# Windowed attention ahead of a gated feed-forward: values of attention in quarters of the array, in two phases round the scores, and two blocks turned at once

## The chip, the cores and the metric

The kernel runs on one core of a Trainium2 chip. The metric is the device time of one execution in microseconds (us), as a median over runs. TensorE (PE in the profile) multiplies matrices, VectorE (DVE) and ScalarE (ACT) work elementwise on 128 partitions, SyncE (SP) issues transfers; each engine goes through its own instructions in order and waits for the others by semaphores. Matmul results land in PSUM, of which a partition has eight banks of 2 KB.

## The reference

Four batches of 768 tokens, 8 heads of 64; each token attends to itself and the 95 before it, and to the first 8 tokens of its sequence. The heads' outputs, 512 wide, go through a gated product and two matrices:

```python
scores = scale * np.matmul(q, k.transpose(0, 1, 3, 2))      # q, k, v: (4, 8, 768, 64), float32
is_global = pos[None, :] < int(n_global)                     # 8
is_local = (rel >= 0) & (rel < int(n_local))                 # 96
bias = -slopes[:, None, None] * dist[None, :, :]
scores = np.where(is_global | is_local, scores + bias[None], -1e9)
scores = scores - np.max(scores, axis=-1, keepdims=True)
a = np.exp(scores)
a = a / (np.sum(a, axis=-1, keepdims=True) + 1e-09)
x = np.matmul(a, v)              # then (3072, 512)
out = ((x @ w1) * (x @ w2) @ w3) @ w_out       # 512 -> 1024 -> 1024 -> 512
```

## The kernel before

**Tiling.** A chunk is 256 tokens (12 in all, 3 to a batch), a block 128 of them (j = 0, 1). Heads go in pairs; u is the head of a pair, and its 64 dimensions are one half of the partitions. A step `s` does two pairs of one chunk, so there are 24 steps. The queries of a block see at most 232 keys: a window of 96 and 8 global ones ahead (104 rows, the "window" piece of the keys), and the block itself (128, the "own" piece). The first block of a batch has no window, so it has only the own piece.

**A step.** PE writes the scores of two pairs (line 406) in 64x64 pieces, which use the four quarters of the array in turn: a half of the rows (u) by a half of the columns (the half g of the block's queries). A piece spans 168 columns, since each half of the queries sees no more; in a batch's first block 64 or 128. DVE adds the bias and takes the rows' extremum (line 421, eight instructions with a read of the accumulator each), ACT makes exponentials and sums (line 422), DVE and ACT scale the rows (lines 427 to 436). PE transposes them (lines 445 and 447) through a PSUM tile of a bank, one block of a pair at a time ("turn", four a step), and ACT copies the result `ph` to SBUF (line 449). PE then multiplies by the values `vr` (457 for the own piece, 459 for the window piece, summed in PSUM). The weights are 64 columns wide, one head's, so a matmul uses all rows (128 or 104) and half the columns. The result `uu`, 128 partitions by two pairs by 256 tokens in one bank, is split into a high part `xh` (ACT, line 63) and the rest `xl` (DVE, line 64). A float32 matmul shows as two records in the trace.

**Visits.** The values of step s - 1 and the scores of step s stand next to one another on PE; that stretch is called visit s here (0 to 24). Between visits PE runs slices of the feed-forward of earlier tokens: a generator (lines 150 to 186) yields after each piece of 6 matmuls, products with w1 and w2 (161 to 163; each in three, high by high, high by low, low by high), then with the folded w3 w_out (178 to 180). ACT evicts the first product (`a`, 168), DVE multiplies (`g`, 171), and ACT and DVE split the product into `gh` and `gl` (63, 64). A new run of the generator begins behind every fourth visit (8, 12, 16, 20; smaller runs before), when 512 tokens are complete.

**What sets the order.** PE's order is written out by hand throughout: the table `SLICES` says how many slices stand between a step's softmax and its turns. In steps 0 to 3 (`first_steps`) DVE's and SP's orders are written by hand too, since the weights are converted from 64-bit floats there (lines 54 to 58, 130, 147) and w3 w_out is folded on PE (142); ACT's order there is the scheduler's. From step 4 on ACT's order is the one in which the code stands, and the scheduler orders DVE and SP.

**PSUM** is full: four banks of scores, one for turns, one for values, two for the feed-forward.

Of the kernel before, what the change touches and what calls it, by code (L numbers as in the profile page):

```python
# [10 lines left out]
F32 = mybir.dt.float32  # L11
F32R = mybir.dt.float32r
BF16 = mybir.dt.bfloat16
I32 = mybir.dt.int32
AF = mybir.ActivationFunctionType
ALU = mybir.AluOpType
PSUM = bass.MemoryType.PSUM

B, H, S, D = 4, 8, 768, 64
DM, DF, DO = 512, 1024, 512  # L20
P = 128
NP = H // 2
NQ = 2
T = NQ * P
NCB = S // T
# [7 lines left out]
BW = WIN + GLB  # L33
UW = BW + P
QW = KW + T
STEP = 2
PC = 512
HF = NFC // 2
HQ = P // 2
# [27 lines left out]
class FeedForward:  # L67
# [25 lines left out]
    def next(self, ring, slots):  # L93
        self.turn[ring] += 1
        return slots[(self.turn[ring] - 1) % len(slots)]
# [229 lines left out]
def banded(ctx, tc, ff, ns, nt, nf, oki, ident, qk, vx):  # L325


    nc = tc.nc
# [3 lines left out]
    ld = ctx.enter_context(tc.tile_pool(name="ld", bufs=STEP))  # L332
    at = ctx.enter_context(tc.tile_pool(name="at", bufs=2))
    ps_s = ctx.enter_context(tc.tile_pool(name="ps_s", bufs=1, space=PSUM))
    ps_t = ctx.enter_context(tc.tile_pool(name="ps_t", bufs=1, space=PSUM))
    ps_v = ctx.enter_context(tc.tile_pool(name="ps_v", bufs=1, space=PSUM))
    sc = [[ps_s.tile([P, NQ, 256], F32, name=f"s{i}{u}") for u in range(2)] for i in range(STEP)]

# [4 lines left out]
    biasw = bp.tile([P, H, UW], BF16, name="biasw")  # L343

    def biases():
        it = at.tile([P, UW], I32, tag="ph", bufs=4, name="it")
        itg = at.tile([P, P], I32, tag="ph", bufs=4, name="itg")
        rel, loc = (at.tile([P, UW], F32, tag="pr", name=n) for n in ("rel", "loc"))

        dist, both0 = ff.t3s[:, 2].bitcast(F32)[:, :UW], ff.t3s[:, 3].bitcast(F32)  # L350
        keep0, dist0 = both0[:, :P], both0[:, P:2 * P]
        own = slice(BW, UW)
        nc.gpsimd.iota(it[:, 0:WIN], pattern=[[-1, WIN]], base=WIN, channel_multiplier=1)
        nc.gpsimd.iota(it[:, WIN:BW], pattern=[[1, GLB]], base=0, channel_multiplier=0)
        nc.gpsimd.iota(it[:, BW:UW], pattern=[[-1, P]], base=0, channel_multiplier=1)
        nc.gpsimd.iota(itg, pattern=[[1, P]], base=0, channel_multiplier=0)
        nc.vector.tensor_copy(out=rel, in_=it)
        nc.vector.tensor_copy(out=keep0, in_=itg)
        nc.vector.tensor_scalar(out=loc, in0=rel, scalar1=0.0, scalar2=None, op0=ALU.is_ge)
        nc.vector.tensor_copy(out=nf, in_=nt)  # L360
        nc.vector.scalar_tensor_tensor(out=loc, in0=rel, scalar=nl, in1=loc, op0=ALU.is_lt, op1=ALU.mult)
        nc.vector.tensor_scalar(out=loc[:, WIN:BW], in0=rel[:, WIN:BW], scalar1=ng, scalar2=None, op0=ALU.is_lt)
        nc.vector.tensor_tensor(out=dist, in0=rel, in1=loc, op=ALU.mult)
        nc.vector.tensor_scalar(out=dist[:, WIN:BW], in0=loc[:, WIN:BW], scalar1=nl, scalar2=None, op0=ALU.mult)

        nc.vector.scalar_tensor_tensor(out=keep0, in0=keep0, scalar=ng, in1=loc[:, own], op0=ALU.is_lt, op1=ALU.max)
        nc.vector.tensor_tensor(out=dist0, in0=keep0, in1=loc[:, own], op=ALU.subtract)
        nc.vector.scalar_tensor_tensor(out=dist0, in0=dist0, scalar=nl, in1=dist[:, own], op0=ALU.mult, op1=ALU.add)
        for d, m in ((dist0, keep0), (dist, loc)):
            nc.vector.tensor_scalar(out=m, in0=m, scalar1=-FAR, scalar2=FAR, op0=ALU.mult, op1=ALU.add)  # L370
            nc.vector.tensor_tensor(out=d, in0=d, in1=m, op=ALU.add)
        for h in range(H):
            sl = -SLOPES[h] / SCALE
            nc.scalar.activation(bias0[:, h, :], dist0, AF.Copy, scale=sl)
            nc.scalar.activation(biasw[:, h, :], dist, AF.Copy, scale=sl)
# [18 lines left out]
    def scores(c, hp, qr):  # L394

        ps = sc[hp % STEP]
        for j in range(NQ):
            w0 = BW if c % NCB == 0 and j == 0 else 0  # L400
            for g in range(P // HQ):
                cols = slice(max(w0, g * HQ), BW + (g + 1) * HQ)
                q0 = KW + j * P + g * HQ
                for u in range(2):
                    m = qr[u * D:(u + 1) * D]
                    nc.tensor.matmul(ps[u][g * HQ:(g + 1) * HQ, j, cols], lhsT=m[:, q0:q0 + HQ], rhs=m[:, j * SLOT:][:, cols], start=True, stop=True)  # L406
        return ps
# [28 lines left out]
                    nc.vector.tensor_scalar(out=x, in0=x, scalar1=r, scalar2=None, op0=ALU.mult)  # L436
        return pr

    def flip(c, hp, j, pr):

        first = c % NCB == 0 and j == 0
        nk = 1 if first else 2
        pt = ps_t.tile([P, 2, 2, P], F32, tag="t", name=f"t_{c}_{hp}_{j}")
        for u in range(2):
            nc.tensor.transpose(pt[:, u, 0], pr[:, j, u, BW:UW], ident)  # L445
            if not first:
                nc.tensor.transpose(pt[:, u, 1], pr[:, j, u, 0:P], ident)  # L447
        ph = at.tile([P, 2, 2, P], F32, tag="ph", bufs=4, name=f"ph_{c}_{hp}_{j}")
        nc.scalar.activation(ph[:, :, :nk], pt[:, :, :nk], AF.Copy)  # L449
        return ph  # L450

    def values(uu, c, hp, vr, phs):
        for j, ph in enumerate(phs):
            first = c % NCB == 0 and j == 0
            for u in range(2):
                rows, o = slice(u * D, (u + 1) * D), uu[u * D:(u + 1) * D, j * P:(j + 1) * P]
                nc.tensor.matmul(o, lhsT=vr[:, j, rows], rhs=ph[:, u, 0], start=True, stop=first)  # L457
                if not first:
                    nc.tensor.matmul(o, lhsT=vr[:BW, 2 * NQ - 1 - j, rows], rhs=ph[:BW, u, 1], start=False, stop=True)  # L459

    n = NC * NP // STEP
    pairs = lambda s: [divmod(STEP * s + i, NP) for i in range(STEP)]
    work = []
    qrs, vrs, phs, xs = {}, {}, {}, {}

    def slices(k):
        while k > 0 and work:
            if next(work[0], "end") == "end":  # L470
                work.pop(0)
            else:
                k -= 1
# [7 lines left out]
    def visit(s):  # L481
        if s:
            c, h0 = pairs(s - 1)[0]
            if h0 == 0 and c % 2 == 0:
                xs[c // 2] = [xp.tile([P, NCC, W], F32R, tag=tag, name=f"{tag}_{c}") for tag in ("xh", "xl")]
            uu = ps_v.tile([P, STEP, T], F32, tag="v", name=f"v_{c}_{h0}")
            for i, p in enumerate(pairs(s - 1)):
                values(uu[:, i], *p, vrs[s - 1][i], phs[s - 1][NQ * i:NQ * (i + 1)])
        ps = [scores(*p, t) for p, t in zip(pairs(s), qrs[s])] if s < n else []
        if s:  # L490
            x2 = xs[c // 2]
            xc = [x[:, :, c % 2 * T:][:, :, :T] for x in x2]
            split(nc, *(x[:, h0:h0 + STEP] for x in xc), uu)
            if h0 + STEP == NP and c < 2:
                work.append(ff.run(c, *xc, c * T, T))
            elif h0 + STEP == NP and c % 2:
                work.append(ff.run(c, *x2, (c - 1) * T, W))
        return ps
# [1 line left out]
    def all_rows(s, ps):  # L500
        return [rows(*p, x) for p, x in zip(pairs(s), ps)]

    def turn(s, m, prs):
        phs.setdefault(s, []).append(flip(*pairs(s)[m // NQ], m % NQ, prs[m // NQ][0]))

    def first_steps():

# [22 lines left out]
        ps = visit(0)  # L530
# [5 lines left out]
        prs = all_rows(0, ps)  # L536
# [12 lines left out]
            loads(s + 1)  # L549

        def fold_and_turn(f, s):
            for m in range(STEP * NQ):
                ff.fold(f, 2 * m, 2 * m + 1)
                turn(s, m, prs)

        w3(3)
        scale(0)
# [9 lines left out]
        prs = all_rows(1, visit(1))  # L567
# [11 lines left out]
        prs = all_rows(2, visit(2))  # L579
# [11 lines left out]
        prs = all_rows(3, visit(3))  # L591
# [4 lines left out]
        w12(7)  # L596
        slices(SLICES[3][0] - 2)
        ff.lows()
        for m in range(STEP * NQ):
            turn(3, m, prs)  # L600
            slices(SLICES[3][m + 1])
        fits(nc, ff.mp, nf, oki)


    SLICES = [()] * 3 + [(4, 2, 2, 1, 1)] * 3 + [(4, 2, 1, 1, 1)] * 2 + [(5, 2, 2, 2, 1)] * (n - 8)
    with tc.manual_schedule(engines={mybir.EngineType.PE}):
        with tc.manual_schedule(engines={mybir.EngineType.DVE, mybir.EngineType.SP}):
            first_steps()
        with tc.manual_schedule(engines={mybir.EngineType.Activation}):
            for s in range(4, n + 1):  # L610
                rs = all_rows(s, visit(s))
                if s == n:
                    break

                slices(2)
                for p, r in zip(pairs(s), rs):
                    softmax(*p, *r, nc.vector)
                loads(s + 1)
                slices(SLICES[s][0] - 2)
                for m in range(STEP * NQ):  # L620
                    turn(s, m, rs)
                    slices(SLICES[s][m + 1])
            slices(10 ** 6)


# [43 lines left out]
```

## Time and profile before

| | before |
|---|---|
| median of 3 runs | 600.2 us |
| lowest and highest run | 599.47, 601.7 us |
| span of the profiled execution, first to last instruction | 597.9 us (the page gives no time of its own beside it) |
| mean granted TensorE clock | 0.997 |
| busy: PE, DVE, ACT | 574.8, 261.2, 287.3 us |
| ACT copies of turned blocks, 128x512 or 128x256 | 96, 53.7 us |

A row of the timeline gives the start and the length of an instruction in us, its engine, line, operation and operands (out <- in), "x4" for four records of a kind in a row, and in brackets how long the engine was idle before it and what released it. The lengths of neighbouring matmuls overlap, since matmuls are pipelined, so a pace is read from starts. A row of the windows gives start and end, the length, and for each engine its busy time and its number of instructions, then the granted clock (1.00 is full), the share of DMA and GB/s. A row of the groups gives a line, an engine, an operation, names and shapes, a count, and after the bar the busy time in us and the mean in ns.

### The profile page before, as it was taken

Reading aid. Unit: us, or ns where it says so; the run is one execution under the profiler, and the core shown is the slowest. Engines: PE = TensorE matmul, PEld = TensorE weight load, DVE = VectorE, ACT = ScalarE, POOL = GpSimd, SP = SyncE. Lnnn points to the kernel's source line nnn. Section 1 sums busy time; section 2 is a strip of 40 time slices with the busy share of each in tenths; the row PEclk is TensorE's granted clock in tenths of the full one; section 3 lists DMA queues with packets and bytes.
Section 4 is the critical chain, followed back from the end, with each engine's and each line's share of the span. In section 5 each row is a group of like instructions: output and inputs, shape, how many; then the busy total and the mean of one; then the engine's idle time right before and its main releaser. Section 6 shows DMA issues by size and latency. Waiting matters only on the chain.

```text
span 597.9 us, 9930 instructions
## 1 busy us (share of the span) xinstructions
PE 574.8 (96%) x3872; PEld 456.3 (76%) x3872; DVE 261.2 (44%) x851; ACT 287.3 (48%) x777; POOL 1.3 (0%) x10
## 2 busy tenths in 40 slices
PE   2998998999999999999999999999999999999995
PEld 0444568989988888888888888888888888888884
DVE  8999998531434425304533322542343453112200
ACT  3065667644556456435635545653553663422210
POOL 0000000000000000000000000000000000000000
PEclk9999999999999999999999999999999999999998
DMA  8896654220132202212211320220331120000011
GB/s 304 296 362 235 218 207 145 81 81 29 52 96 97 77 3 79 81 37 81 79 43 36 115 98 18 62 64 2 123 105 37 42 80 19 36 18 1 0 37 40
DMA packets 23240, 54.01 MB, mean 90 GB/s; under 512 B 2704, under 2 KB 4752, under 8 KB 23184
## 3 DMA queue, kind: packets, MB, share of 16 engines
q1 hardware_dynamic: 23184, 53.29, 26.2%
q8 instruction: 32, 0.52, 0.4%
q14 instruction: 24, 0.20, 0.1%
HBM read 46.99 MB, written 6.29 MB: 89 GB/s over the span
## 4 chain that ended last, share of the span: by engine, by line
PE 84%; DVE 10%; DMA 3%; ACT 1%; issue 0%; SPq 0%; DVEq 0%; ACTq 0%
PE m L161 15%; PE m L163 14%; PE m L162 14%; PE o L178 8%; PE o L180 7%; PE o L179 7%; PE s L406 4%; PE v L457 4%; PE t L445 3%; PE v L459 3%; PE t L447 3%; PE w L142 2%; DVE t L56 1%; DVE t L58 1%; DMA stage<-w3t 1%; DMA raws<-w 1%
## 5 line engine op out<-in xcount | busy, mean ns | idle before, releaser
L422 ACT ACTIVATE pr<-pr,mx 128x232 f32<-128x232 f32 (+1 forms) x192 | 88.4, 462 | 48.1 <-DVE mx L421 48.1
L449 ACT ACTIVATE ph<-t 128x512 f32<-128x512 f32 (+1 forms) x96 | 53.7, 560 | 88.3 <-PE t L447 81.1
L171 DVE TENSOR_TENSOR g<-m,a 128x512 f32<-128x512 f32 x48 | 33.2, 691 | 133.4 <-PE m L163 132.7
L161 PE MATMUL m<-xh,w1h 128*128 128x512 f32 (+1 forms) x224 | 84.5, 377 | 0.0
L161 PE MATMUL m<-xh,w2h 128*128 128x512 f32 (+1 forms) x224 | 83.0, 371 | 0.5 <-ACT a L168 0.5
L163 PE MATMUL m<-xh,w2l 128*128 128x512 f32 (+1 forms) x224 | 80.7, 360 | 0.0
L163 PE MATMUL m<-xh,w1l 128*128 128x512 f32 (+1 forms) x224 | 80.6, 360 | 0.0
L162 PE MATMUL m<-xl,w1h 128*128 128x512 f32 (+1 forms) x224 | 80.5, 360 | 0.0
L162 PE MATMUL m<-xl,w2h 128*128 128x512 f32 (+1 forms) x224 | 80.5, 359 | 0.0
L178 PE MATMUL o<-wh,gh 128*128 128x512 f32 x192 | 78.2, 407 | 0.0
L180 PE MATMUL o<-wh,gl 128*128 128x512 f32 x192 | 75.2, 392 | 0.0
L179 PE MATMUL o<-wl,gh 128*128 128x512 f32 x192 | 75.0, 390 | 0.0
L142 PE MATMUL w<-wo,t 128*128 128x512 f32 x128 | 60.7, 619 | 12.3 <-DVE wo L58 11.2
L64 DVE TENSOR_TENSOR xl<-v,xh 128x512 fp32r<-128x512 f32 x24 | 16.6, 690 | 122.5 <-ACT xh L63 122.5
L63 ACT ACTIVATE gh<-g 128x512 fp32r<-128x512 f32 x48 | 30.3, 630 | 68.0 <-DVE g L171 67.2
L142 PEld LDWEIGHTS w<-wo,t 128*128 128x128 f32 x128 | 24.0, 197 | 39.9 <-issue 21.7
L421 DVE CUSTOM_DVE_ANT_0 pr<-s,biasw 128x232 f32<-128x232 f32 x160 | 53.4, 394 | 0.0
L445 PE MATMUL t<-ident,pr 128*128 128x128 f32 x192 | 45.9, 274 | 4.0 <-ACT pr L434 3.4
L161 PEld LDWEIGHTS m<-xh,w1h 128*128 128x128 f32 x224 | 42.2, 189 | 8.5 <-issue 3.3
L161 PEld LDWEIGHTS m<-xh,w2h 128*128 128x128 f32 x224 | 42.3, 189 | 7.0 <-issue 0.7
L163 PEld LDWEIGHTS m<-xh,w1l 128*128 128x128 f32 x224 | 42.2, 189 | 6.6
L163 PEld LDWEIGHTS m<-xh,w2l 128*128 128x128 f32 x224 | 42.2, 189 | 6.5
(84 smaller groups left out, 807.0 us busy)
## 6 DMA issues: line engine op xcount, KB each, us to landing
qr<-qk SPq DMA_DIRECT2D x32, 312.0 KB, 4.2
vr<-vx SPq DMA_DIRECT2D x32, 256.0 KB, 3.1
stage<-w3t SPq DMA_DIRECT2D x15, 512.0 KB, 6.2
out_dram<-ot SPq DMA_DIRECT2D x24, 256.0 KB, 2.0
raws<-w SPq DMA_DIRECT2D x10, 512.0 KB, 5.6
qr<-qk SPq DMA_DIRECT2D x16, 260.0 KB, 3.5
vr<-vx SPq DMA_DIRECT2D x16, 192.0 KB, 2.6
stage<-w SPq DMA_DIRECT2D x6, 512.0 KB, 6.8
```

The source lines that it names most:

```text
L142: nc.tensor.matmul(ps, lhsT=self.t3[f, z][:, i * P:(i + 1) * P].bitcast(F32), rhs=self.wo[:, k].bitcast(F32), start=k == 0, stop=k == NFC - 1)
L161: nc.tensor.matmul(ps[:, z], lhsT=mh, rhs=xh[:, i], start=i == 0, stop=False)
L162: nc.tensor.matmul(ps[:, z], lhsT=mh, rhs=xl[:, i], start=False, stop=False)
L163: nc.tensor.matmul(ps[:, z], lhsT=ml, rhs=xh[:, i], start=False, stop=i == NCC - 1)
L171: nc.vector.tensor_tensor(out=g, in0=ps, in1=a, op=ALU.mult)
L178: nc.tensor.matmul(ps, lhsT=gh[:, f, ts], rhs=self.wh[:, f], start=f == 0, stop=False)
L179: nc.tensor.matmul(ps, lhsT=gh[:, f, ts], rhs=self.wl[:, f], start=False, stop=False)
L180: nc.tensor.matmul(ps, lhsT=gl[:, f, ts], rhs=self.wh[:, f], start=False, stop=f == NFC - 1)
L421: nc.vector.tensor_tensor_reduce(out=pr[:, j, u, w0:], in0=ps[u][:, j, w0:UW], in1=bias, scale=-SCALE, scalar=3.0e38, op0=ALU.add, op1=ALU ...
L422: nc.scalar.activation(pr[:, j, u, w0:], pr[:, j, u, w0:], AF.Exp, bias=m, scale=-1.0, accum_out=sm[:, j, u:u + 1])
L445: nc.tensor.transpose(pt[:, u, 0], pr[:, j, u, BW:UW], ident)
L449: nc.scalar.activation(ph[:, :, :nk], pt[:, :, :nk], AF.Copy)
```

## The change

**Values in quarters.** `values` (now line 478) takes pieces of 64 rows of `vr` by one head's 64 columns, so it uses the four quarters of the array as the scores do. A phase k has the row half g = i XOR k for pair i: in phase 0 the first pair uses the upper rows and the second pair the lower ones, in phase 1 the other way round. The two row halves never write into one bank at the same time, as each pair now has a bank of its own (`uv` is 128 x 2 x 512, of which 256 columns a pair hold values). A row half of keys whose probabilities are zero for a half of the queries is left out there: such pieces have 64 columns. A full visit has 16 pieces with 128 columns and 16 with 64, where it had 16 matmuls with 128. Phase 0 stands before the scores of the next step and phase 1 behind them. Between the phases ACT writes a 128x2 tile into the unused column behind the values (line 513); it waits for phase 0, and phase 1 waits for it. The last visit, which has no scores, does the values as before.

**Turns.** The bank of the turns is gone: turned blocks go through the two banks of the values. Both blocks of a pair are transposed into one tile of 128 x 1024 and copied by one ACT instruction (line 450; a batch's first chunk has two, 448 and 450). So a step has two turns where it had four, and `SLICES` and the folding of the first steps are regrouped, with the same sums.

```diff
-    ps_t = ctx.enter_context(tc.tile_pool(name="ps_t", bufs=1, space=PSUM))
...
-    def flip(c, hp, j, pr):
...
+    def flip(c, hp, pr, ph):
+        pt = ps_v.tile([P, NQ * 2, 2, P], F32, tag="v", name=f"t_{c}_{hp}")
+        for j in range(NQ):
             first = c % NCB == 0 and j == 0
             for u in range(2):
+                nc.tensor.transpose(pt[:, NQ * j + u, 0], pr[:, j, u, BW:UW], ident)
                 if not first:
+                    nc.tensor.transpose(pt[:, NQ * j + u, 1], pr[:, j, u, 0:P], ident)
+            if first:
+                nc.scalar.activation(ph[:, :2, 0], pt[:, :2, 0], AF.Copy)
+        m0 = 2 if c % NCB == 0 else 0
+        nc.scalar.activation(ph[:, m0:], pt[:, m0:], AF.Copy)
...
+    def values(uu, s, k):
+        ps, todo = pairs(s), []
+        for j in range(NQ):
+            first = ps[0][0] % NCB == 0 and j == 0
+            for part in range(1 if first else 2):
+                for i in range(STEP):
+                    g = k if k == 2 else i ^ k
+                    win = part if k == 2 else 0 if first else part ^ g
+                    if k == 2 or g == win:
+                        cut = [(0, HQ), (HQ, HQ)] if first and k == 1 else [(0, P)]
+                    else:
+                        cut = [(g * HQ, HQ)]
+                    todo += [(i, u, j, win, g, q, n) for q, n in cut for u in range(2)]
+        for m, (i, u, j, win, g, q, n) in enumerate(todo):
+            x = views(s, i, NQ * j + u)[win]
+            step = P // x.shape[1]
+            v = vrs[s][i][:, 2 * NQ - 1 - j if win else j, u * D:(u + 1) * D]
+            r = slice(g % 2 * HQ, BW if g and win else P if g else HQ)
+            others = [t[:2] == (i, u) for t in todo]
+            nc.tensor.matmul(uu[u * D:(u + 1) * D, i, j * P + q:j * P + q + n], lhsT=v[r], rhs=x[:, q // step:(q + n) // step][r],
+                             start=k != 1 and not any(others[:m]), stop=k > 0 and not any(others[m + 1:]))
...
-            uu = ps_v.tile([P, STEP, T], F32, tag="v", name=f"v_{c}_{h0}")
-            for i, p in enumerate(pairs(s - 1)):
-                values(uu[:, i], *p, vrs[s - 1][i], phs[s - 1][NQ * i:NQ * (i + 1)])
+            uv = ps_v.tile([P, STEP, 512], F32, tag="v", name=f"v_{c}_{h0}")
+            uu = uv[:, :, :T]
+            values(uu, s - 1, 0 if s < n else 2)
         ps = [scores(*p, t) for p, t in zip(pairs(s), qrs[s])] if s < n else []
         if s:
+            if s < n:
+                nc.scalar.activation(uv[:, :, T], ident[:, :STEP], AF.Copy)
+                values(uu, s - 1, 1)
...
-            for m in range(STEP * NQ):
-                ff.fold(f, 2 * m, 2 * m + 1)
-                turn(s, m, prs)
+            for i in range(STEP):
+                ff.fold(f, *range(HF * i, HF * (i + 1)))
+                turn(s, i, prs)
...
-    SLICES = [()] * 3 + [(4, 2, 2, 1, 1)] * 3 + [(4, 2, 1, 1, 1)] * 2 + [(5, 2, 2, 2, 1)] * (n - 8)
+    SLICES = [()] * 3 + [(5, 3, 2)] * 3 + [(5, 2, 2)] * 2 + [(6, 4, 2)] * (n - 8)
```

The order of the instructions moves at three places. The first is the end of visit 17 on PE (values of chunk 8's pairs 0 and 1, scores `s` of its pairs 2 and 3, then the feed-forward's products `m`). Before:

```order
L406 MATMUL s10_106<-qr_8_3_3491 64x168
L406 MATMUL s11_107<-qr_8_3_3491 64x168
L161 MATMUL m_7_3_0_3665<-xh_6_2826,w1h_74 128x512
L162 MATMUL m_7_3_0_3665<-xl_6_2827,w1h_74 128x512
L163 MATMUL m_7_3_0_3665<-xh_6_2826,w1l_75 128x512
```

and after the change:

```order
L405 MATMUL s11_104<-qr_8_3_3664 64x168
L478 MATMUL v_8_0_3775<-ph_8_0_3702,vr_8_0_3462 64x128 x2
L478 MATMUL v_8_0_3775<-ph_8_1_3745,vr_8_1_3464 64x128 x2
L478 MATMUL v_8_0_3775<-ph_8_0_3702,vr_8_0_3462 64x64 x2
L478 MATMUL v_8_0_3775<-ph_8_1_3745,vr_8_1_3464 64x64 x2
L478 MATMUL v_8_0_3775<-ph_8_0_3702,vr_8_0_3462 64x128 x2
L478 MATMUL v_8_0_3775<-ph_8_1_3745,vr_8_1_3464 64x128 x2
L478 MATMUL v_8_0_3775<-ph_8_0_3702,vr_8_0_3462 64x64 x2
L478 MATMUL v_8_0_3775<-ph_8_1_3745,vr_8_1_3464 64x64 x2
L161 MATMUL m_7_3_0_3849<-xh_6_2951,w1h_74 128x512
L162 MATMUL m_7_3_0_3849<-xl_6_2952,w1h_74 128x512
```

Phase 1, eight rows of two pieces for the two blocks, stands where the feed-forward followed on the scores; the other eight (phase 0) stand ahead of the scores, where all sixteen stood.

The second is DVE at visit 16, where a run of the feed-forward begins (`xl` is the low part of the values, `pr` the rows of the softmax). Before:

```order
L64 TENSOR_TENSOR xl_6_2827<-v_7_2_3403,xh_6_2826 128x2x256
L421 ISA pr_8_0_3438,mx_8_0_3439<-s00_104,biasw_109 128x232
L421 ISA mx_8_0_3439 128x1
L421 ISA pr_8_0_3438,mx_8_0_3439<-s01_105,biasw_109 128x232
L421 ISA mx_8_0_3439 128x1
```

and after the change, the last two of them shown with what follows:

```order
L420 ISA pr_8_1_3622,mx_8_1_3623<-s10_103,biasw_106 128x232
L420 ISA mx_8_1_3623 128x1
L420 ISA pr_8_1_3622,mx_8_1_3623<-s11_104,biasw_106 128x232
L420 ISA mx_8_1_3623 128x1
L64 TENSOR_TENSOR xl_6_2952<-v_7_2_3559,xh_6_2951 128x2x256
L426 TENSOR_SCALAR sm_8_0_3613<-sm_8_0_3613 128x4
```

The subtraction `xl` stood ahead of the eight reductions of the next step and now stands behind them; so it does from visit 4 on, while in visits 1 to 3 it stays ahead.

The third is ACT at visit 2, in the start (`w1h` and `w2h` are high parts of weights, `wh` one of the folded weights). Before:

```order
L122 ACTIVATE w1h_74<-t3s_116 128x512
L144 ACTIVATE wh_78<-w_5_518 128x512
L449 ACTIVATE ph_0_3_1_550<-t_0_3_1_545 128x512
L122 ACTIVATE w2h_76<-t3s_116 128x512
L63 ACTIVATE xh_0_409<-v_0_2_565 128x2x256
```

and after the change:

```order
L122 ACTIVATE w1h_74<-t3s_113 128x512
L144 ACTIVATE wh_78<-w_5_526 128x512
L448 ACTIVATE ph_0_3_546<-t_0_3_547 128x2x128
L122 ACTIVATE w2h_76<-t3s_113 128x512
L450 ACTIVATE ph_0_3_546<-t_0_3_547 128x512
L513 ACTIVATE v_0_2_569<-ident_58 128x2
L63 ACTIVATE xh_0_402<-v_0_2_569 128x2x256
```

The copy of the larger turned block moved behind `w2h`, and the small write between the phases stands ahead of `xh`.

More of the change, by code (lines that the diff above doesn't have):

```diff
@@ L345, in biases @@
     def biases():
-        it = at.tile([P, UW], I32, tag="ph", bufs=4, name="it")
-        itg = at.tile([P, P], I32, tag="ph", bufs=4, name="itg")
+        it = at.tile([P, UW], I32, tag="ph", name="it")
+        itg = at.tile([P, P], I32, tag="ph", name="itg")
         rel, loc = (at.tile([P, UW], F32, tag="pr", name=n) for n in ("rel", "loc"))
@@ L437, in softmax @@
         return pr
-    def flip(c, hp, j, pr):
[L441 to L450, printed above, removed]
@@ L452, in values @@
-    def values(uu, c, hp, vr, phs):
-        for j, ph in enumerate(phs):
+    def flip(c, hp, pr, ph):
+        pt = ps_v.tile([P, NQ * 2, 2, P], F32, tag="v", name=f"t_{c}_{hp}")
+        for j in range(NQ):
             first = c % NCB == 0 and j == 0
             for u in range(2):
-                rows, o = slice(u * D, (u + 1) * D), uu[u * D:(u + 1) * D, j * P:(j + 1) * P]
-                nc.tensor.matmul(o, lhsT=vr[:, j, rows], rhs=ph[:, u, 0], start=True, stop=first)
+                nc.tensor.transpose(pt[:, NQ * j + u, 0], pr[:, j, u, BW:UW], ident)
@@ L458, in values, with views @@
                 if not first:
-                    nc.tensor.matmul(o, lhsT=vr[:BW, 2 * NQ - 1 - j, rows], rhs=ph[:BW, u, 1], start=False, stop=True)
+                    nc.tensor.transpose(pt[:, NQ * j + u, 1], pr[:, j, u, 0:P], ident)
[3 more added lines that the diff above has]
+        nc.scalar.activation(ph[:, m0:], pt[:, m0:], AF.Copy)
+    def views(s, i, m):
+        ph = phs[s][i]
+        return ph[:, m, 0], ph[:, m, 1]
@@ L501, in all_rows, with turn @@
         return [rows(*p, x) for p, x in zip(pairs(s), ps)]
-    def turn(s, m, prs):
-        phs.setdefault(s, []).append(flip(*pairs(s)[m // NQ], m % NQ, prs[m // NQ][0]))
+    def turn(s, i, prs):
+        c, hp = pairs(s)[i]
+        phs.setdefault(s, []).append(at.tile([P, NQ * 2, 2, P], F32, tag="ph", name=f"ph_{c}_{hp}"))
+        flip(c, hp, prs[i][0], phs[s][i])
     def first_steps():
@@ L598, in first_steps @@
         ff.lows()
-        for m in range(STEP * NQ):
-            turn(3, m, prs)
-            slices(SLICES[3][m + 1])
+        for i in range(STEP):
+            turn(3, i, prs)
+            slices(SLICES[3][i + 1])
         fits(nc, ff.mp, nf, oki)
-    SLICES = [()] * 3 + [(4, 2, 2, 1, 1)] * 3 + [(4, 2, 1, 1, 1)] * 2 + [(5, 2, 2, 2, 1)] * (n - 8)
+    SLICES = [()] * 3 + [(5, 3, 2)] * 3 + [(5, 2, 2)] * 2 + [(6, 4, 2)] * (n - 8)
     with tc.manual_schedule(engines={mybir.EngineType.PE}):
@@ L619, in banded @@
                 slices(SLICES[s][0] - 2)
-                for m in range(STEP * NQ):
-                    turn(s, m, rs)
-                    slices(SLICES[s][m + 1])
+                for i in range(STEP):
+                    turn(s, i, rs)
+                    slices(SLICES[s][i + 1])
             slices(10 ** 6)
```

## The prediction

> **What bounds the kernel now.** I read the page first: busy time, then the chain that ended last.
>
> ```profile
> span 597.9 us, 9930 instructions
> ...
> PE 574.8 (96%) x3872; PEld 456.3 (76%) x3872; DVE 261.2 (44%) x851; ACT 287.3 (48%) x777; POOL 1.3 (0%) x10
> ...
> PE 84%; DVE 10%; DMA 3%; ACT 1%; issue 0%; SPq 0%; DVEq 0%; ACTq 0%
> ```
>
> TensorE (PE) carries 84% of the chain, VectorE (DVE) 10%. Where DVE does is told by the busy time of each stretch:
>
> ```profile
> 0.00:100.80 100.80, 84.27 (x456) 46.52 (x456) 95.57 (x245) 53.65 (x155) 1.32 (x10) 1.00 0.72 262
> ...
> 184.00:526.00 342.00, 342.00 (x2356) 280.60 (x2352) 122.47 (x464) 177.02 (x479) 0.00 (x0) 1.00 0.19 61
> ```
>
> The columns are length, then PE, weight loads, DVE, ACT, POOL, then the granted clock. Up to 100.8 us DVE is busy for 95.57 and converts the weights; from 184 on PE never idles (342.00 of 342.00) at clock 1.00. So after the start a microsecond of PE is a microsecond of the kernel, and before it PE time is worth nothing and DVE's is.
>
> Next the stretch that the change rewrites, PE's visits. Each window runs from the start of the last feed-forward matmul ahead of a visit to the start of the second one behind it:
>
> ```profile
> 373.86:377.79 3.93, 3.93 (x68) 1.00 0.24 54
> 395.58:399.38 3.80, 3.80 (x68) 1.00 0.24 64
> 437.36:440.85 3.49, 3.49 (x60) 1.00 0.44 128
> 416.71:420.06 3.35, 3.35 (x59) 1.00 0.38 115
> 523.81:526.43 2.62, 2.62 (x35) 1.00 0.26 97
> ```
>
> The first has full values and scores, the second a batch's first scores, the third a batch's first values (24 records, not 32), the fourth both first, the last values alone. Of the 20 visits from 4 to 23, 14 have full values and 6 a batch's first. Inside the first window the timeline of PE has
>
> ```profile
> 373.86 0.40 PE L163 MATMUL m<-xh,w2l 128*128 128x512 f32 x1
> 374.19 0.45 PE L457 MATMUL v<-ph,vr 128*64 128x128 f32 x4
> 374.46 0.40 PE L459 MATMUL v<-ph,vr 104*64 104x128 f32 x4
> ...
> 375.78 0.44 PE L459 MATMUL v<-ph,vr 104*64 104x128 f32 x4
> 376.15 1.37 PE L406 MATMUL s<-qr 64*64 64x168 f32 x32
> 377.45 0.50 PE L161 MATMUL m<-xh,w1h 128*128 128x512 f32 x1
> ```
>
> **PE's visits, step by step.** From 374.46 to 375.78 there are six groups of four value records in 1.32 us: 0.22 a group. Two column halves of the array work at once, so a round of two records with 128 columns takes 0.11, and 32 records 1.76. The change makes 64 records of them, four at once: 16 rounds, 8 with 128 columns and 8 with 64 (the halves whose other columns are masked to zero are skipped). The 128-column rounds take 8 x 0.11 = 0.88. The price of a 64-column round is seen where a batch's first scores have such pieces (line 406 alone; by shape, then all of its records by window):
>
> ```profile
> L406 PE MATMUL s<-qr 64*64 64x64 f32 x2 | 0.2, 216 | 0.0
> ...
> L406 PE MATMUL s<-qr 64*64 64x64 f32 x4 | 0.3, 217 | 0.0
> ```
>
> ```profile
> 418.99:419.02 0.03, 0.03 (x12) 1.00 0.38 137
> 418.99:419.08 0.09, 0.09 (x14) 1.00 0.94 364
> 418.99:419.14 0.15, 0.15 (x18) 1.00 1.06 410
> ```
>
> The first group is 419.005 to 419.02, the second to 419.075: two 64-column records start by 419.02, two more by 419.08, and by 419.14 the next ones of all four quarters have started. So a 64-column round takes at most 0.07, and half of 0.11, 0.055, fits. From below it cannot be less than its columns, 0.055; from above it is bounded by a 128-column round, 0.11. I take 0.055: 8 x 0.055 = 0.44, together 1.32, so **-0.44** for a full visit. With a batch's first values 24 records now take 12 x 0.11 = 1.32 (the third window is 0.44 shorter than the first, which is four rounds); their phases take 0.55 each, 1.10, so -0.22.
>
> The last group of values starts at 375.78 and the scores at 376.15: 0.37, of which 0.22 is the group. The 0.15 left is the change of the array's shape, from columns in halves to quarters. Values in quarters have the scores' shape, so it goes: **-0.15**. The entry from 128x128 (0.33 from 373.86 to 374.19) and the exit stay.
>
> Phase 1 waits for the 128x2 write on ACT that stands between the phases, and that for phase 0. Around it ACT has
>
> ```profile
> 375.09 0.63 ACT L63 ACTIVATE gh<-g 128x512 fp32r<-128x512 f32 x1 [1.60 <-DVE g L171]
> 376.26 0.60 ACT L63 ACTIVATE xh<-v 128x512 fp32r<-128x512 f32 x1 [0.54 <-PE v L459]
> ...
> 378.38 0.19 ACT L422 ACTIVATION_READ_ACCUMULATOR pr<-pr,mx 128x1 f32 x1
> ```
>
> No row has a 128x2 ACT write; the nearest by size is the 128x1 read, 0.19. The scores cover it: phase 0 ends at 374.19 + 0.66 = 374.85, the scores take 377.45 - 376.15 = 1.30 with the exit or some 1.14 without, to 375.99. The write is queued behind gh, which ends at 375.72, so it ends at 375.91, just in time; where gh comes later, phase 1 waits. If the cover were gone, each visit would pay gh's lateness and 0.19, some 0.25. For the semaphore I take +0.05 a visit (0 to 0.15, a shape change), and +0.5 in all for three visits in which gh is late (0 to 1.0).
>
> Sum: full visits 14 x (-0.44 - 0.15 + 0.05) = -7.6; first ones 6 x (-0.22 - 0.15 + 0.05) = -1.9; gh +0.5. **PE: -9.0.**
>
> The transposes of a step stay sixteen, in two groups of eight for four of four, and ACT's copies become two of 128x1024 for four of 128x512, which take 0.59 (a row is shown at the start, below), so at most 2 x 0.59 = 1.18 each. The copy now empties the bank that the values use too, so the second pair's transposes wait for the first copy, and the next values for the second. Two or more slices of feed-forward stand between, 12 matmuls at a pitch of 0.23 (357.45 to 357.68 below): 2.7 us against 1.2. I cost this at nothing; without the slices it would be some microsecond a group.
>
> The loads of the values now wait for phase 1, and the loads queue behind one another on SP:
>
> ```profile
> qr<-qk SPq DMA_DIRECT2D x32, 312.0 KB, 4.2
> vr<-vx SPq DMA_DIRECT2D x32, 256.0 KB, 3.1
> ```
>
> They land in 4.2 and 3.1 us, and a step is 373.86 - 352.14 = 21.7 long, so half a microsecond later costs nothing.
>
> **The run starts.** Every fourth step a new feed-forward run begins right behind the visit (8, 12, 16, 20), and its eighth matmul reads the fresh xl. DVE has xl ahead of the eight row reductions now, and behind them after the change:
>
> ```profile
> 355.17 0.69 DVE L64 TENSOR_TENSOR xl<-v,xh 128x512 fp32r<-128x512 f32 x1 [15.69 <-ACT xh L63]
> 355.78 0.39 DVE L421 CUSTOM_DVE_ANT_0 pr<-s,biasw 128x232 f32<-128x232 f32 x1
> ...
> 358.01 0.39 DVE L421 CUSTOM_DVE_ANT_0 pr<-s,biasw 128x232 f32<-128x232 f32 x1
> ```
>
> ```profile
> 352.14 0.40 PE L180 MATMUL o<-wh,gl 128*128 128x512 f32 x1
> ...
> 357.45 0.39 PE L162 MATMUL m<-xl,w1h 128*128 128x512 f32 x1
> 357.68 0.39 PE L163 MATMUL m<-xh,w1l 128*128 128x512 f32 x1
> ```
>
> A reduction takes 0.32 (seven from 355.78 to 358.01). The first pair's scores would end about 352.14 + 0.33 + 0.66 + 0.57, and 0.3 for the last record's length, at 354.0; eight reductions bring 356.6, and xl 357.3. The eighth matmul would be due at 357.45 - 0.54 = 356.9: PE waits 0.4. In two of the others the saving ahead is less or alike (0.5 each), in the fourth a batch's first rows are shorter and it fits: **+1.4** (0 to 2.5). In the other visits xl is read only steps later, and its place costs nothing.
>
> **The start.** In visits 1 to 3 PE's savings are worth nothing. The in-order DVE waits for xl there, and xh now needs phase 1, behind the scores, and on ACT the bigger copy of the transposes behind the weight copy w2h:
>
> ```profile
> 67.32 0.59 ACT L449 ACTIVATE ph<-t 128x512 f32<-128x512 f32 x1
> 67.80 0.63 ACT L122 ACTIVATE w2h<-t3s 128x512 fp32r<-128x512 f32 x1
> 68.68 0.60 ACT L63 ACTIVATE xh<-v 128x512 fp32r<-128x512 f32 x1 [0.26 <-PE v L459]
> ```
>
> ```profile
> 69.67 0.68 DVE L64 TENSOR_TENSOR xl<-v,xh 128x512 fp32r<-128x512 f32 x1
> ...
> 100.15 0.69 DVE L171 TENSOR_TENSOR g<-m,a 128x512 f32<-128x512 f32 x1
> ```
>
> ```profile
> 100.84 0.39 PE L161 MATMUL m<-xh,w2h 128*128 128x256 f32 x1 [0.46 <-ACT a L168]
> ```
>
> ```profile
> 70.27:100.15 29.88, 28.49 (x192) 19.66 (x190) 28.49 (x82) 23.88 (x66) 0.00 (x0) 1.00 0.61 219
> ```
>
> With w2h first, ph would end near 68.9; phase 0 (0.55), scores (1.14) and phase 1 (0.55) end at 71.2, xh at 71.8, xl starts 2.1 to 2.4 later than 69.67. From there DVE is busy for 28.49 of 29.88, so little is made up; visit 3 adds some tenths. What waits for DVE and for ACT behind it at 100 us, PE's 100.84 with it, comes later by about **+2.7** (+1.0, if the 1.39 idle takes up the rest, to +3.5).
>
> **Sum.** -9.0 + 1.4 + 2.7 = -4.9 against the span of 597.9: 593.0. The page shows the span alone; the median of the runs is 600.2, 2.3 above it. With the same 2.3 the time is **595.3**.
>
> **Rivals.** (a) The waits are absorbed: nothing lost at the start and the run starts. For it: DVE's idle 1.39, and PE has its own work to catch up there; against it: both queues run in order. 600.2 - 9.0 - 0.4, about 591.
>
> (b) A 64-column round costs what a 128-column one does, 0.11, since something other than columns sets its pace. Then 8 rounds cost 0.44 more in each of 20 visits, +8.8: 595.3 + 8.8 = 604.1, slower than before. It decides from 0.055 + 0.055 x 4.9 / 8.8 = 0.086 a round. Against it stand the at most 0.07 of the first scores; for it, that those pieces ran beside longer ones.
>
> In the Trainium skill, TensorE: Matmul & The Clock Gate, "LDWEIGHTS" and "The mechanism" of Part 3, a weight load takes its columns over 1.2 GHz and overlaps a running matmul only in another row group. By that, an estimate, a load of 64 columns (0.053) would come on top of each record in a quarter, and a 64-column round would cost 0.11 as here in (b). The trace does not bear it out for long: records of 128 columns, which all take the same rows, run at 0.11 a round with no load beside them.
>
> (c) The phases wait for each other in every visit, 0.25 by the cover's reckoning above: 20 x 0.25 = 5.0, so 600.3, no change. For it: a margin of 0.08 in the visit shown; against it: only where gh stands just ahead on ACT.
>
> (d) The quarters of two pairs do not overlap: then 16 rounds become 32 and the values 1.3 a visit longer, 20 x 1.3 = +26, 621. The scores' 32 records in 1.30 speak against it.
>
> **Chances.** The forecast 0.55, with a range of its own from 592.5 to 598; (a) 0.15; (b) 0.10; (c) 0.17; (d) 0.03. Runs of this kernel differ by about 0.5%, so faster is under 597.2 and slower above 603.2. Faster is 0.48 of the forecast's 0.55 and (a), 0.63 in all; the rest of the forecast, (c) but 0.02 and a little of (b) make 0.25 for no change; (b), (d) and the 0.02 are 0.12 with what is left over. The range leaves out (d), most of (b) and the faster end of (a): 590.5 to 602.
>
> **What would show it.** Right: a full visit of 3.4 where it was 3.93; 64-column values at half the pitch of 128; no gap between values and scores; xl at visit 2 near 72 and PE's first full stretch from about 103.5, not 100.84; waits of PE for xl of about half a microsecond in three run starts. Wrong: visits at 3.8 (b), PE waiting for ACT ahead of phase 1 in most visits (c), or PE resuming at 101 (a). The forecast fails in size if DVE's order at the run starts makes `a` or the rows late as well, which I cost at nothing.

## The result, and the profile after

| | before | after the change |
|---|---|---|
| median | 599.99 us (4 runs, 599.47 to 601.7) | 603.62 us (4 runs, 602.5 to 604.67) |
| span of the profiled execution | 597.9 us | 602.9 us |
| ratio, 95% interval | | 1.0055 (1.0034 to 1.0076) |

The kernel became slower by about half a per cent, where 595.3 us was forecast. Of the four executions of the changed kernel two took 604.67 (the profiled one) and 604.32 us at a mean clock of 0.994, and two 602.5 and 602.93 at 0.999 and 0.998. The page of the changed kernel:

```profile
span 602.9 us, 11349 instructions
...
PE 566.4 (94%) x4576; PEld 454.2 (75%) x4576; DVE 261.8 (43%) x851; ACT 283.0 (47%) x768; POOL 1.3 (0%) x10
...
PE 84%; DVE 9%; ACT 3%; DMA 2%; issue 1%; SPq 0%; ACTq 0%; DVEq 0%
```

PE is busy for 8.4 us less than before (574.8), and yet the end comes 5.0 later. So the matmuls did become cheaper, and PE stands still for longer. The visits first, in the same windows as those of before (last feed-forward matmul ahead to the second one behind; full, a batch's first scores, first values, both, and the last visit):

```profile
379.27:382.58 3.31, 3.31 (x99) 1.00 0.16 24
400.33:403.50 3.17, 3.17 (x100) 1.00 0.14 33
444.01:447.07 3.06, 3.06 (x87) 1.00 0.33 100
422.42:425.35 2.93, 2.93 (x88) 1.00 0.35 107
528.77:531.33 2.56, 2.56 (x35) 1.00 0.25 94
```

Each is 0.42 to 0.63 shorter than it was (3.93, 3.80, 3.49, 3.35), but for the last, whose values stay whole: it is 0.06 shorter, and its pieces now stand in another order and go to two banks. Over visits 4 to 23 the savings add up to 11.1 us. Inside the full visit the timeline of PE is

```profile
379.27 0.39 PE L163 MATMUL m<-xh,w2l 128*128 128x512 f32 x1
379.59 0.90 PE L478 MATMUL v<-ph,vr 64*64 64x128 f32 x32
380.31 1.33 PE L405 MATMUL s<-qr 64*64 64x168 f32 x32
381.45 0.86 PE L478 MATMUL v<-ph,vr 64*64 64x128 f32 x32
382.24 0.50 PE L161 MATMUL m<-xh,w1h 128*128 128x512 f32 x1
```

with no gap at either border: values, scores and values follow one another at the pace of their rounds. Where the time went is in the list of what PE waited for (in total, times, longest):

```profile
PE w L142 <- DVE wo L58: 11.7, 2, 11.3
PE t L444 <- ACT ph L448: 10.9, 16, 1.1
PE v L478 <- ACT ph L450: 2.8, 3, 1.1
PE m L162 <- DVE xl L64: 1.4, 3, 0.5
PE m L161 <- DVE g L171: 1.4, 1, 1.4
```

The first row was there before (11.2). The second is new: sixteen times a transpose waits for the small copy of a turned block (line 448). In the list of before a transpose waits for a copy (line 449 there) once:

```profile
PE t L445 <- ACT ph L449: 0.3, 1, 0.3
```

Sixteen is the number of turns in the four first chunks of a batch, where the first block has no window and is copied by an instruction of its own, between its two transposes and the four of the second block. One of them on PE and on ACT:

```profile
282.08 0.38 PE L444 MATMUL t<-ident,pr 128*128 128x128 f32 x2
283.20 0.33 PE L444 MATMUL t<-ident,pr 128*128 128x128 f32 x1 [0.74 <-ACT ph L448]
283.37 0.27 PE L446 MATMUL t<-ident,pr 128*128 128x128 f32 x1
```

```profile
282.27 0.60 ACT L168 ACTIVATE a<-m 128x512 f32<-128x512 f32 x1 [1.29 <-PE m L163]
282.77 0.38 ACT L448 ACTIVATE ph<-t 128x256 f32<-128x256 f32 x1
```

The third transpose starts 283.20 - 282.19 = 1.01 us after the second, where transposes follow at 0.11: ACT evicts `a` first, then copies, and only when the copy has ended (282.77 + 0.38 = 283.15) does PE go on. Nothing of the feed-forward stands in between, so PE loses 0.9. By the code the transposes that wait write the second half of the tile, and the copy reads the first half alone, so no value that they need is missing; why the program has them wait was not tried.

The span can be cut at the starts of visits 4 and 24. Before:

```profile
0.00:107.44 107.44, 90.86 (x511) 1.00 0.68 246
107.44:523.81 416.37, 416.09 (x3043) 1.00 0.20 63
```

and after the change:

```profile
0.00:112.37 112.37, 91.01 (x599) 0.98 0.66 235
112.37:528.77 416.40, 407.56 (x3658) 1.00 0.20 63
```

The start is 4.9 longer. Its mean clock is 0.98: in this execution the clock of PE fell for a short while there (last section). The widened run among the experiments has the same order, with the clock at 1.00 in the start, and begins visit 4 at 111.40:

```profile
0.00:111.40 111.40, 90.68 (x600) 1.00 0.66 237
```

So about 1.0 of the 4.9 belongs to the clock, and 4.0 to the change. The long middle takes the same 416.4, though its matmuls need 8.5 less: the visits' 11.1 are spent on waits. The experiments take these two apart.

### The profile page after: what moved, and what is told of

Read it like the earlier page. It is cut to its first block, busy times and chain, and to the rows that moved or that the text cites. A ratio compares the mean times of both kernels' runs of the same rounds, so it can differ in the third digit from the quotient of the medians.

```text
span 602.9 us, 11349 instructions
## 1 busy us (share of the span) xinstructions
PE 566.4 (94%) x4576; PEld 454.2 (75%) x4576; DVE 261.8 (43%) x851; ACT 283.0 (47%) x768; POOL 1.3 (0%) x10
## 4 chain that ended last, share of the span: by engine, by line
PE 84%; DVE 9%; ACT 3%; DMA 2%; issue 1%; SPq 0%; ACTq 0%; DVEq 0%
PE m L161 14%; PE m L162 14%; PE m L163 14%; PE o L178 7%; PE o L179 7%; PE o L180 7%; PE v L478 6%; PE s L405 4%; PE w L142 4%; PE t L444 4%; PE t L446 3%; DVE pr L420 2%; DMA stage<-w3t 1%; DVE t L56 1%; DVE t L58 1%; ACT ph L448 1%
## 5 line engine op out<-in xcount | busy, mean ns | idle before, releaser
L161 PE MATMUL m<-xh,w1h 128*128 128x512 f32 (+1 forms) x224 | 82.6, 369 | 0.3 <-ACT a L168 0.3
L178 PE MATMUL o<-wh,gh 128*128 128x512 f32 x192 | 76.7, 399 | 0.0
L142 PE MATMUL w<-wo,t 128*128 128x512 f32 x128 | 58.7, 610 | 12.2 <-DVE wo L58 11.7
L450 ACT ACTIVATE ph<-t 128x1024 f32<-128x1024 f32 (+1 forms) x48 | 42.4, 883 | 43.8 <-PE t L446 43.8
L162 PEld LDWEIGHTS m<-xl,w1h 128*128 128x128 f32 x224 | 42.3, 189 | 8.9 <-DVE xl L64 3.2
L168 ACT ACTIVATE a<-m 128x512 f32<-128x512 f32 x48 | 28.4, 592 | 41.9 <-PE m L163 41.9
```

Source lines behind the costliest of these rows:

```text
L142: nc.tensor.matmul(ps, lhsT=self.t3[f, z][:, i * P:(i + 1) * P].bitcast(F32), rhs=self.wo[:, k].bitcast(F32), start=k == 0, stop=k == NFC - 1)
L161: nc.tensor.matmul(ps[:, z], lhsT=mh, rhs=xh[:, i], start=i == 0, stop=False)
L162: nc.tensor.matmul(ps[:, z], lhsT=mh, rhs=xl[:, i], start=False, stop=False)
L178: nc.tensor.matmul(ps, lhsT=gh[:, f, ts], rhs=self.wh[:, f], start=f == 0, stop=False)
L450: nc.scalar.activation(ph[:, m0:], pt[:, m0:], AF.Copy)
```

## The experiments

The first four ran together, beside the kernel before at 599.5 us.

**The late copy.** Two lines change places, so that the small copy stands on ACT behind all six transposes:

```diff
         for j in range(NQ):
...
-            if first:
-                nc.scalar.activation(ph[:, :2, 0], pt[:, :2, 0], AF.Copy)
         m0 = 2 if c % NCB == 0 else 0
+        if m0:
+            nc.scalar.activation(ph[:, :2, 0], pt[:, :2, 0], AF.Copy)
         nc.scalar.activation(ph[:, m0:], pt[:, m0:], AF.Copy)
```

> The changed kernel, but in a batch's first chunk the copy of the first block stands on ACT behind all six transposes of the pair, not between the second and the third. Theory W (the time was lost in PE's waits for that small copy in the middle of a turn, about 0.9 us in each of 12 turns from step 6 on, and some in the four turns of the start): PE's waits of the transposes for the small copy fall from 10.9 us to about 0, the time from 603.6 to about 592.5 (590 to 595). Rival B (the turns share the banks of the values, and it is this sharing that PE pays for, so the wait only moves to the next reader of the bank): 602 to 604. Rival S (the start alone costs what was lost): 600 to 603.

Measured: 589.01 us (588.9 to 589.86), 0.9827 of before (0.9811 to 0.9844). The turn at the same place of the program now has its transposes in one go, and the feed-forward right behind them:

```profile
273.73 0.49 PE L444 MATMUL t<-ident,pr 128*128 128x128 f32 x3
274.05 0.27 PE L446 MATMUL t<-ident,pr 128*128 128x128 f32 x1
274.16 0.27 PE L444 MATMUL t<-ident,pr 128*128 128x128 f32 x1
274.27 0.27 PE L446 MATMUL t<-ident,pr 128*128 128x128 f32 x1
274.30 0.48 PE L161 MATMUL m<-xh,w2h 128*128 128x512 f32 x1
```

No wait of a transpose for a copy is left in its list, and the values wait for copies as before (3.1 us for 2.8). Its stretches are

```profile
0.00:107.05 107.05, 89.31 (x600) 1.00 0.69 247
107.05:513.36 406.31, 404.89 (x3659) 1.00 0.20 65
```

The middle is 10.1 shorter than in the changed kernel, 0.84 for each of its 12 turns. The start is 5.3 shorter, 1.0 of it by the clock; the 4.3 left are more than I expected of four turns. It now ends 0.4 before that of the old kernel. With these two lines the change is a gain of 1.7%.

**Values alone.** The values in quarters and phases, with the turns of before, one block at a time, through the shared banks and with the old table of slices:

```diff
-        pt = ps_v.tile([P, NQ * 2, 2, P], F32, tag="v", name=f"t_{c}_{hp}")
+        pt = ps_v.tile([P, 2, 2, P], F32, tag="v", name=f"t_{c}_{hp}_{j}")
...
-    SLICES = [()] * 3 + [(5, 3, 2)] * 3 + [(5, 2, 2)] * 2 + [(6, 4, 2)] * (n - 8)
+    SLICES = [()] * 3 + [(4, 2, 2, 1, 1)] * 3 + [(4, 2, 1, 1, 1)] * 2 + [(5, 2, 2, 2, 1)] * (n - 8)
```

> The changed kernel with the turns of before: one block of a pair at a time, four turns a step with the old table of slices, but through the shared banks of the values. So the values in quarters and in phases are there, the merging of the turns is not. Theory W: no wait inside a turn is left, and slices stand between the turns; 592 to 594, as in the run with the late copy. Rival B: the shared bank now has four turns a step to pass instead of two, so as slow as the changed kernel or slower, 603 to 606.

Measured: 595.5 us (595.37 to 596.66), 0.9938 of before (0.9921 to 0.9954). Faster than before, so sharing the banks is not what cost; but above what theory W gave. From visit 4 to 24 it needs 408.2, 1.9 more than with merged turns, and its visit 4 begins at 111.55, 4.5 later. So merged turns are worth something that I had costed at nothing: 1.9 in the middle. The 4.5 in the start is not their price alone. The clock fell in this run's start too (0.73, 0.50 and 0.92 in the three windows of 2 us from 40 to 46), which by these figures is up to 1.7 us of PE's time, an estimate.

**The values of before, with merged turns.** The phases are left out:

```diff
-            values(uu, s - 1, 0 if s < n else 2)
+            values(uu, s - 1, 2)
...
-            if s < n:
-                nc.scalar.activation(uv[:, :, T], ident[:, :STEP], AF.Copy)
-                values(uu, s - 1, 1)
```

> The changed kernel with the values of before: all rows by half the columns, all of them ahead of the scores, and no write between phases; the turns of a pair stay merged, in the shared banks. Theory W: PE's visits are as long as before (3.93 full), which gives back the 11.3 us that the quarters save; DVE has xl ahead of the rows again (1.4 less), and the values of visits 1 to 3 end before the scores (some 2 to 3 less in the start): 603.6 + 11.3 - 1.4 - 2.5 = 611 (608 to 614), with PE's waits for the small copy at 10 to 11 us. Rival S: the start is what costs, and is cured here: 605 to 608.

Measured: 609.54 us (608.74 to 611.03), 1.0172 of before (1.0152 to 1.0193), as theory W had it; PE waits for the small copy for 10.6 us here too. The visits give back 9.8 of the 11.1 and not all: a full one takes 3.86, not 3.93. Its pieces keep the changed kernel's order and two banks, which may be why. Later the same kernel ran with the late copy:

> The whole-values run (values as before, ahead of the scores; turns of a pair merged; 609.5) with the late copy besides: the merged turns alone, without the wait in their middle. Theory W says the wait costs the same whatever the values do, 10.1 from visit 4 on and 5.3 in the start between the changed kernel and the late-copy one, so 609.5 - 14.6 to 15.4 = 594.5; and that the merged turns themselves save what separates the late-copy run from the run by block (6.5, of which 4.5 in the start): 599.5 - 6.5 = 593. If the merged turns save nothing of their own and what was gained belongs to the pair of edits: 599 to 600.

Measured: 595.4 us (595.14 to 595.77), 0.9928 of before (0.9909 to 0.9948). The late copy saves 14.1 here and 14.6 with the phases. From visit 4 to 24 that is 10.2 here (423.37 to 413.19) and 10.1 there, so the wait costs the same in the middle whatever the values do; in the start it costs 3.2 here (visit 4 at 109.85 and 106.62) and 4.3 there. Without the wait, merged turns save 4.3 (0.0072 of 600), of which 1.3 is the shorter whole visits (3.86); visit 4 begins 0.8 earlier than before. Values alone save 4.0, with the clock's fall in that run, and both together 10.5, about 2 more than the sum.

**Half-width pieces at full width.**

```diff
-                        cut = [(g * HQ, HQ)]
+                        cut = [(0, P)]
```

> The changed kernel with every piece of 64 columns that a mask allowed widened to 128 columns (the added products are zero); the pieces of a batch's first block stay. It prices the half-width pieces. By columns (0.055 a round of 64, 0.11 of 128): 8 more rounds' halves in a full visit, 0.44, in 14 visits, and 4, 0.22, in 6: +7.5 us, 611. If a round costs the same at both widths: no change, 603 to 604.

Measured: 609.71 us (609.49 to 609.83), 6.1 above the changed kernel. A full visit is

```profile
382.12:385.83 3.71, 3.71 (x99) 1.00 0.17 24
```

0.40 longer than 3.31 for 8 rounds that went from 64 columns to 128, 0.05 a round. A first one went from 3.06 to 3.27, 0.21 for four rounds. In all 14 x 0.40 + 6 x 0.21 = 6.9, where the forecast had 7.5 and the medians differ by 6.1: the changed kernel's median holds some of the clock's fall. So a round of 64 columns costs about half of one of 128, as the forecast took it, and rival (b) falls, although the changed kernel ended near its 604.1.

The next four started from the late copy, beside the kernel before at 599.65.

**Whole values in visits 1 to 3.**

```diff
-            values(uu, s - 1, 0 if s < n else 2)
+            values(uu, s - 1, 0 if 4 <= s < n else 2)
...
-            if s < n:
+            if 4 <= s < n:
```

> The kernel with the late copy (589.0), but in visits 1 to 3 the values stay whole and ahead of the scores as before; the phases begin with visit 4. Theory P (phase 1 behind the scores makes xh and xl late in the start, where DVE works in order without idle time; the merged turns and the regrouped folds gave back as much, so that the late-copy kernel reaches visit 4 at 107.05 and the one before at 107.44): visit 4 begins at about 104.5, 2.5 earlier, as between the whole-values run (109.85) and the changed kernel (112.37), and the time is 586.5. Rival (the start is bound by the transfers and conversions of the weights, and the values' place there counts for nothing): visit 4 at 107, 589.

Measured: 588.7 us (588.57 to 588.94), 0.9812 of before (0.9795 to 0.9829), against 0.9827 (0.9811 to 0.9844) for the late copy: not to be told apart. Visit 4 begins at 106.63, 0.4 earlier, not 2.5. Theory P falls: that phase 1 stands behind the scores is worth almost nothing in the start, once no turn waits in its middle. Of the 2.5 on which it built, 1.0 was the clock; the other 1.5 (109.85 to 111.40) is what the place costs while the turns do wait.

**Both phases ahead of the scores.** The small write and phase 1 move up behind phase 0:

```diff
             values(uu, s - 1, 0 if s < n else 2)
+            if s < n:
+                nc.scalar.activation(uv[:, :, T], ident[:, :STEP], AF.Copy)
+                values(uu, s - 1, 1)
         ps = [scores(*p, t) for p, t in zip(pairs(s), qrs[s])] if s < n else []
         if s:
-            if s < n:
-                nc.scalar.activation(uv[:, :, T], ident[:, :STEP], AF.Copy)
-                values(uu, s - 1, 1)
```

> The late-copy kernel with both phases ahead of the scores, one behind the other with the small ACT write between: it prices the place of phase 1. PE then stands still from the end of phase 0 until ACT has written. From the rows of ACT (0.19 for a small read, and the length of the last records, 0.25) some 0.5 a visit: 20 x 0.5 = 10, so 599 (595 to 602), with xl ahead of the rows less 1.4 and the start a little better. If the small write costs next to nothing: 588 to 589.

Measured: 605.41 us (604.1 to 606.79), 16.4 above the late copy and beyond the range. PE's list now has

```profile
PE v L478 <- ACT v L510: 12.2, 23, 1.1
PE v L478 <- ACT ph L450: 6.2, 3, 4.1
```

The first row is the place's price: a visit takes 3.88 where nothing holds ACT and 4.27 where gh stands ahead of the write, for 3.31: 0.57 and 0.96 more, where some 0.5 was forecast. The second has one wait of 4.1 at visit 2, in the start, which I had not foreseen. In the changed kernel the scores cover this write: its list has no wait of PE for it.

**DVE in the order of the code, xl ahead everywhere.**

```diff
-        with tc.manual_schedule(engines={mybir.EngineType.Activation}):
+        with tc.manual_schedule(engines={mybir.EngineType.Activation, mybir.EngineType.DVE}):
```

> The late-copy kernel with DVE in the order of the code from step 4 on too, so that xl stands ahead of the row reductions in every visit, as before. PE's three waits for xl, 1.4 in all, go. But the rows start behind xh and xl, about 2.4 later in a visit than in the late-copy kernel and some 0.7 later than in the kernel before, measured from the visit's start. If a margin stays in the chain of rows, exponentials and the eviction of the first product: 587.6. If that eviction now comes last, PE waits some tenths in each of 20 visits: 590 to 595.

Measured: 597.24 us (596.92 to 597.83), 8.2 above the late copy and above the range. From visit 4 to 24 it takes 414.32, 8.0 longer, where PE's visible waits grow from 1.4 to 5.3; the rest was not followed. Then xl ahead at the run starts alone, on the kernel with whole values in visits 1 to 3:

```diff
-                rs = all_rows(s, visit(s))
+                with tc.manual_schedule(engines={mybir.EngineType.DVE if s % 4 == 0 and 8 <= s < n else mybir.EngineType.Activation}):
+                    rs = all_rows(s, visit(s))
```

> The kernel of the whole values in visits 1 to 3, and besides xl ahead of the row reductions in the four visits where a run of the feed-forward begins (8, 12, 16, 20) and only there; nothing else moves on any engine. PE's three waits for xl (0.5 each) go: 1.4 less than that kernel, 585. If a wait for the eviction of the first product takes their place, no less.

Measured: 589.17 us (588.98 to 590.3), 0.9822 of before (0.9803 to 0.9841): no less. PE's list of the late copy, of the run in the order of the code, and of this one have, in this order,

```profile
PE m L162 <- DVE xl L64: 1.4, 3, 0.5
```

```profile
PE m L161 <- ACT a L168: 5.1, 10, 0.6
```

```profile
PE m L161 <- ACT a L168: 2.6, 4, 1.0
```

The wait for xl goes, and one for the eviction of the first product takes its place. Of the last row's 2.6, one wait of 1.0 lies in the start, where the run that it set out from has it too; the other three are the run starts'. With xl ahead the row reductions start late, the exponentials behind them too, and on ACT the eviction stands behind these: at visit 16 the exponentials begin 1.67 behind the start of xh in this run (348.46, 350.13) and 0.49 with the late copy (348.39, 348.88). The scheduler's order, which lets xl wait, is the better one when all visits are taken, and no worse at the run starts.

## Why the prediction was wrong, step by step

**The step that failed** is the one on the turns: "The copy now empties the bank that the values use too [...] Two or more slices of feed-forward stand between [...] I cost this at nothing." I looked for who waits between turns and found them covered, as they are. I did not look inside a turn. In the first chunk of a batch a pair's turn has two copies, as the change itself says, and the program has the second block's transposes wait for the first one. Before, the two blocks had tiles and turns of their own, with slices between. The cover of the old place was lost by joining the two, and the price is 0.84 in each of 12 turns, 10.1 in all, and 4.3 in the start, with the clock's 1.0 taken off: the late copy shows both. The changed kernel ended 3.6 above the one before, the late copy 10.5 below, where the sum said 4.9 below: without the wait the rest of the sum was 5.6 too dear, 2.1 of it in PE's visits and 3.1 in the start, as follows. That the merged turns by themselves gain 1.9 in the middle was in no term either; 1.5 of it is lost again between the visits once the values are in phases, and where was not followed. No rival had this mechanism.

**PE's visits** were right in mechanism and a little too small in size: forecast -0.54 and -0.32, measured -0.62 and -0.42 or -0.43 (-0.32 in visit 13, where gh is late), in all -11.1 for -9.0. The 64-column round is as priced (0.05 by the widened run). The gap to the scores went, and no new one came at phase 1, where I had allowed 0.05 a visit, nor did gh's lateness cost more than 0.1, in visit 13, for the 0.5 allowed.

**The run starts** came out at three waits of half a microsecond, 1.4, the number forecast. But this is not a price that could be had back, as the last run shows: there PE waits for the eviction instead.

**The start** was forecast at +2.7 and measured at +4.9, or +4.0 without the clock's fall, and its mechanism was in the main wrong. xl at visit 2 was late, at 74.39 for 69.67, later still than the 72 of the forecast; but with the late copy it is at 69.07, phases and all. The changed kernel, the widened run (clock at 1.00) and the late copy:

```profile
74.39 0.69 DVE L64 TENSOR_TENSOR xl<-v,xh 128x512 fp32r<-128x512 f32 x1 [2.77 <-ACT xh L63]
```

```profile
73.06 0.69 DVE L64 TENSOR_TENSOR xl<-v,xh 128x512 fp32r<-128x512 f32 x1 [3.03 <-ACT xh L63]
```

```profile
69.07 0.69 DVE L64 TENSOR_TENSOR xl<-v,xh 128x512 fp32r<-128x512 f32 x1 [0.32 <-ACT xh L63]
```

Between 36 and 107 us DVE waits 5.1 us for xh in the changed kernel, 4.4 in the widened run, and 1.3 with the late copy:

```profile
DVE xl L64 <- ACT xh L63: 5.1, 3, 2.8
```

```profile
DVE xl L64 <- ACT xh L63: 4.4, 2, 3.0
```

```profile
DVE xl L64 <- ACT xh L63: 1.3, 2, 1.0
```

Most of what I had put down to the place of phase 1 came from the wait in the turns ahead of it: the place costs 1.5 with that wait and 0.4 without. Why the start is 4.5 later with turns by block than with merged ones stays open: with whole values the merged turns begin visit 4 only 0.8 earlier than the kernel before, the clock's fall is in the 4.5, and no run separates the merging from the regrouping of the folds.

**The rivals.** (a) was half right: with the late copy the start costs nothing, while the run starts do cost. (b) gave the right time for the wrong reason, which is luck. (c) and (d) fall: PE's list has no wait for the write, and the quarters overlap, as the visits' 3.31 shows. The Trainium skill's sentence in (b), from TensorE: Matmul & The Clock Gate, "The mechanism" of Part 3, that a weight load overlaps only in another row group, is not what the time shows here. Phase 0 of the visit above has eight rounds in 380.31 - 379.59 = 0.72, where the columns need 4 x 0.11 + 4 x 0.055 = 0.66; a load of 0.053 on top of each round, by the skill's figure, would make it 1.08, an estimate. In the trace each record of values does have a load of its own (384 of line 457 before, 135 ns each, longer still than the skill's figure), so the loads run beside the matmuls. The same section also has loads pulled ahead into a background weight buffer, which the prediction left out.

## What to carry to other kernels

Where two transfers or turns are joined into one, look at what is still separate inside: a small instruction on another engine in the middle of a group on the engine that bounds the kernel costs a whole round trip, here 0.84 us on average, and what covered it stays outside the group. Put the small instructions behind the group. And a wait that is removed on a chain with little margin is worth nothing until the next wait on that chain is known, as xl and the eviction of the first product show.

## What the runs showed of the hardware

In the profiled execution of the changed kernel, the clock of PE fell for a short while in the start, though PE never stood still for more than 1.1 us at a time in the 8 us ahead of the fall:

```profile
44.00:48.00 4.00, 2.96 (x11) 1.00 0.18 66
48.00:50.00 2.00, 1.28 (x39) 0.81 0.86 309
50.00:52.00 2.00, 2.00 (x49) 0.50 0.73 226
52.00:54.00 2.00, 2.00 (x17) 0.84 0.86 270
```

```profile
45.80:49.20 3.40, 1.64 (x27) 1.00 0.30 98
49.20:50.00 0.80, 0.80 (x29) 0.53 1.03 399
```

The columns are length, busy time of PE, then the granted clock. The fall comes at about 49.2, behind 3.4 us in which PE was busy for 1.64. Visit 1, from the last transpose ahead of it (47.43) to the second fold matmul behind it (53.12), took 5.69 there, and 4.10 with the late copy at clock 1.00. Twice more the clock fell in a start, behind a longer standstill: behind 4.09 us in the run with both phases ahead (0.69, 0.50 and 0.96 in the three windows of 2 us from 70) and behind 2.45 us in the run with turns by block.

In the Trainium skill, TensorE: Matmul & The Clock Gate, "What's actually happening", the clock halves after an idle window of about 3.4 us; here a window that was only half idle was enough. But the widened run went through a like stretch in the same order without a fall:

```profile
45.60:49.00 3.40, 1.79 (x25) 1.00 0.37 119
```

What decided between the two is open.
